# Decode attention on one core: one head at a time in shared 4 MB slots, V stationary in the value matmul, wq loaded first and wo last

## The chip, the cores and the metric

The kernel runs on one core of a Trainium2 chip. The metric is the device time in microseconds of one execution, the median of several. All runs quoted here are of the state "fast" unless it is said otherwise. Clocks, waits and packet times come from the one run of each kernel that was profiled. Abbreviations: PE is TensorE, PEld its weight loads, DVE is VectorE, ACT is ScalarE, POOL is GpSimd, SP is SyncE, which only issues loads here. "PEclk" is the clock that TensorE was granted, as a share of full speed.

## The reference, cut to what matters

```python
def reference(x, k_cache, v_cache, wq, wo, w1, w2, w3, w4):   # names shortened
    # B=2, Sq=1, D=512; Hq=32 query heads, Hkv=8 key heads (rep=4), Sk=32768, Dh=128, F=1792
    xn = layernorm(x)
    q  = (xn @ wq).reshape(B, 1, 32, 128)
    p  = softmax(q . k_cache * 128**-0.5)          # per head, over 32768 keys
    s  = (p @ v_cache) @ wo
    h2 = gelu(layernorm(xn) @ w3) @ w4             # the w1/w2 part shifts its one row away
    return x + s * silu(xn + h2)
```

K and V are 268.4 MB of bf16. Every element is used once for four query rows, so the kernel is a stream of loads with a little arithmetic behind each of them. One thing about correctness has to be known: the attention output is so small beside x that the comparison with the reference says little about the attention part.

## The kernel before

Heads are handled in pairs, and K and V arrive in tiles of 4096 tokens: 1 MB, 8 KB in a row on each of 128 partitions.

```python
NC_MAX = 4096; GPS = 2; TPB = 8        # tokens per tile, heads at a time, K tiles per PSUM tile
KN_BUFS = 5; V_BUFS = 6
...
kn = kn_pool.tile([128, TPC, 128], BF16, tag="kn", name=f"kn{j}")
k_eng.dma_start(out=kn[:, :, :],
    in_=A_k_cache[b, g, c * NC:(c + 1) * NC, :].rearrange("(p t) d -> p t d", p=128))
...
for c in range(NCHUNK + 1):
    # 1. transpose K of chunk c on TensorE, copy PSUM to SBUF (DVE 3 of 4, ACT 1 of 4)
    nc.tensor.transpose(out=tTs[j][:, i, :], in_=kns[j][:, u, :], identity=ident[:, :])
    ...
    # 2. PV of chunk c-1: exp columns stationary (4), V moving (128 columns), two heads in turn
    nc.tensor.matmul(o_ps[j][32 * j:32 * j + rep, 0:Dh],
        lhsT=pep[j][:, u * rep:(u + 1) * rep], rhs=pvt[j][:, u, :],
        start=first, stop=last, tile_position=(0, 32 * j))
    ...
    # 3. scores of chunk c: K^T stationary, q moving (4 columns); then exp on ACT
    nc.tensor.matmul(scs[j][:, u * rep:(u + 1) * rep],
        lhsT=ktbs[j][blk][:, i, :], rhs=q4[j], start=True, stop=True)
```

wq, w3 and w4 are loaded after the first K and V tiles, wo in two halves in the second and third of eight sets of heads; wq and wo in rows of 1 KB.

The softmax here doesn't subtract the row's maximum and nothing guards it: scores larger than these inputs give would overflow.

Of the kernel before, what the change touches and what calls it, by code (L numbers as in the profile page):

```python
# [8 lines left out]
F32 = mybir.dt.float32  # L10
BF16 = mybir.dt.bfloat16
ACT = mybir.ActivationFunctionType
ALU = mybir.AluOpType

NC_MAX = 4096
GPS = 2
TPB = 8
KN_BUFS = 5
V_BUFS = 6
KT_BUFS = 12  # L20
EP_BUFS = 4
TT_BUFS = 3
SC_BUFS = 2
O_BUFS = 2
# [3 lines left out]
def kernel(  # L28
# [13 lines left out]
    dbg: bass.AP | None = None,  # L42
# [9 lines left out]
    assert Sq == 1 and Dh == 128 and rep == 4 and D % 128 == 0 and Fdim % 128 == 0  # L52
    assert Hkv % GPS == 0
    DK = D // 128
    FK = Fdim // 128
    NC = min(NC_MAX, Sk)
    assert Sk % NC == 0
    TPC = NC // 128
    assert TPC % TPB == 0
    NBLK = TPC // TPB  # L60
    NCHUNK = Sk // NC
    eps = 1e-5
    inv_sqrt_dh = float(Dh) ** -0.5
    GELU_C = 0.7978845608028654

    n_sets = B * (Hkv // GPS)

    pers = ctx.enter_context(tc.tile_pool(name="pers", bufs=1))
    kn_pool = ctx.enter_context(tc.tile_pool(name="kn", bufs=KN_BUFS))
    v_pool = ctx.enter_context(tc.tile_pool(name="vpool", bufs=V_BUFS))  # L70
    pro_ps = ctx.enter_context(tc.tile_pool(name="pro_ps", bufs=1, space=bass.MemoryType.PSUM))
    tT_psp = ctx.enter_context(tc.tile_pool(name="tT_ps", bufs=TT_BUFS, space=bass.MemoryType.PSUM))
    sc_psp = ctx.enter_context(tc.tile_pool(name="sc_ps", bufs=SC_BUFS, space=bass.MemoryType.PSUM))
    o_psp = ctx.enter_context(tc.tile_pool(name="o_ps", bufs=O_BUFS, space=bass.MemoryType.PSUM))

    def set_groups(s):
        b = s // (Hkv // GPS)
        g0 = (s % (Hkv // GPS)) * GPS
        return b, [g0 + j for j in range(GPS)]

    def issue_chunk_dma(s, c, k_eng=None, v_eng=None):
        b, groups = set_groups(s)
        k_eng = k_eng or nc.sync
        v_eng = v_eng or nc.sync
        kns, vts = [], []
        for j in range(GPS):
            g = groups[j]
            kn = kn_pool.tile([128, TPC, 128], BF16, tag="kn", name=f"kn{j}")
            k_eng.dma_start(
                out=kn[:, :, :],  # L90
                in_=A_k_cache[b, g, c * NC:(c + 1) * NC, :].rearrange("(p t) d -> p t d", p=128),
            )
            kns.append(kn)
        for j in range(GPS):
            g = groups[j]
            vt = v_pool.tile([128, TPC, 128], BF16, tag="v", name=f"vt{j}")
            v_eng.dma_start(
                out=vt[:, :, :],
                in_=A_v_cache[b, g, c * NC:(c + 1) * NC, :].rearrange("(p t) d -> p t d", p=128),
            )  # L100
            vts.append(vt)
        return kns, vts

    x_bf = pers.tile([B, D], BF16)
    nc.sync.dma_start(out=x_bf[:, :], in_=A_x[:, 0, :])

    first_dma = issue_chunk_dma(0, 0, k_eng=nc.sync, v_eng=nc.sync)
# [4 lines left out]
    def layernorm(dst_f32, src_f32, tagp):  # L112
        stats = pers.tile([B, nc.vector.BN_STATS_DIM], F32, name=f"stats_{tagp}")
        nc.vector.bn_stats(out=stats[:, :], in_=src_f32[:, :])
        mv = pers.tile([B, nc.vector.BN_AGGR_DIM], F32, name=f"mv_{tagp}")
        nc.vector.bn_aggr(out=mv[:, :], in_=stats[:, :])
        rstd = pers.tile([B, 1], F32, name=f"rstd_{tagp}")
        nc.vector.tensor_scalar_add(out=rstd[:, :], in0=mv[:, 1:2], scalar1=eps)
        nc.scalar.activation(out=rstd[:, :], in_=rstd[:, :], func=ACT.Sqrt)
        nc.vector.reciprocal(out=rstd[:, :], in_=rstd[:, :])  # L120
        nc.vector.tensor_scalar(
            out=dst_f32[:, :], in0=src_f32[:, :],
            scalar1=mv[:, 0:1], scalar2=rstd[:, 0:1],
            op0=ALU.subtract, op1=ALU.mult,
        )
# [10 lines left out]
    ident = pers.tile([128, 128], BF16)  # L136
    make_identity(nc, ident[:, :])
    ones_f = pers.tile([128, 1], F32)
    nc.gpsimd.memset(ones_f[:, :], 1.0)

    treg = pro_ps.tile([128, 2 * DK * B], BF16, tag="pro")
    for k in range(DK):
        nc.tensor.transpose(out=treg[:, k * B:k * B + B], in_=xn_bf[0:B, k * 128:(k + 1) * 128], identity=ident[0:B, 0:B])  # L143
        nc.tensor.transpose(out=treg[:, (DK + k) * B:(DK + k) * B + B], in_=ln2_bf[0:B, k * 128:(k + 1) * 128], identity=ident[0:B, 0:B])
    xT = pers.tile([128, 2 * DK, B], BF16)
    nc.vector.tensor_copy(out=xT[:, :, :], in_=treg[:, :].rearrange("p (k b) -> p k b", b=B))

    wo_sb = pers.tile([128, Hq, D], BF16)
    w3_sb = pers.tile([128, DK, Fdim], BF16)
    w4_sb = pers.tile([128, FK, D], BF16)  # L150
# [4 lines left out]
    o_sb = pers.tile([36, Dh], BF16)  # L155
    nc.gpsimd.memset(o_sb[:, :], 0.0)
    s_acc = [pers.tile([128, rep], F32, name=f"s_acc{j}") for j in range(GPS)]

    QPH = 4 if Hq % 4 == 0 else 2
    NQP = Hq // QPH  # L160
    wq3 = A_wq.rearrange("(k p) f -> p k f", p=128)
    wqp = tc.alloc_tile_pool(name="wq_pool", bufs=NQP)
    qT_ps = pro_ps.tile([128, Hq * B], F32, tag="pro")
    for hp in range(NQP):
        wq_sb = wqp.tile([128, DK, QPH * Dh], BF16, tag="wq")
        nc.sync.dma_start(out=wq_sb[:, :, :], in_=wq3[:, :, hp * QPH * Dh:(hp + 1) * QPH * Dh])  # L166
        for hh in range(QPH):
            h = hp * QPH + hh
            for k in range(DK):
                nc.tensor.matmul(  # L170
                    qT_ps[:, h * B:(h + 1) * B],
                    lhsT=wq_sb[:, k, hh * Dh:(hh + 1) * Dh],
                    rhs=xT[:, k, :],
                    start=(k == 0), stop=(k == DK - 1),
                )
    nc.vector.tensor_copy(out=q_sb[:, :, :], in_=qT_ps[:, :].rearrange("p (h b) -> p b h", b=B))  # L176
    wqp.release()
    nc.sync.dma_start(out=w3_sb[:, :, :], in_=B_w3.rearrange("(k p) f -> p k f", p=128))
    nc.sync.dma_start(out=w4_sb[:, :, :], in_=B_w4.rearrange("(f p) d -> p f d", p=128))

    kt_pool = ctx.enter_context(tc.tile_pool(name="ktb", bufs=KT_BUFS))
    ep_pool = ctx.enter_context(tc.tile_pool(name="ep", bufs=EP_BUFS))
    rec_pool = ctx.enter_context(tc.tile_pool(name="rec", bufs=4))
    part_pool = ctx.enter_context(tc.tile_pool(name="part", bufs=4))

    def emit_mlp_branch():
        hT_ps = pro_ps.tile([128, FK * B], F32, tag="pro")
        for f in range(FK):
            for k in range(DK):
                nc.tensor.matmul(  # L190
                    hT_ps[:, f * B:(f + 1) * B],
                    lhsT=w3_sb[:, k, f * 128:(f + 1) * 128],
                    rhs=xT[:, DK + k, :],
                    start=(k == 0), stop=(k == DK - 1),
                )
        hf = pers.tile([128, FK * B], F32)
        nc.vector.tensor_copy(out=hf[:, :], in_=hT_ps[:, :])
# [10 lines left out]
        h2_ps = pro_ps.tile([B, D], F32, tag="pro")  # L208
        for f in range(FK):
            nc.tensor.matmul(  # L210
                h2_ps[0:B, :],
                lhsT=h_bf[:, f * B:(f + 1) * B],
                rhs=w4_sb[:, f, :],
                start=(f == 0), stop=(f == FK - 1),
            )
        t_f = pers.tile([B, D], F32)
        nc.vector.tensor_add(out=t_f[:, :], in0=xn[:, :], in1=h2_ps[0:B, :])
# [4 lines left out]
    emit_mlp_branch()  # L222

    for s in range(n_sets):
        b, groups = set_groups(s)
        wo3 = A_wo.rearrange("(h p) d -> p h d", p=128)
        if s == min(1, n_sets - 1):
            nc.sync.dma_start(out=wo_sb[:, 0:Hq // 2, :], in_=wo3[:, 0:Hq // 2, :])
        if s == min(2, n_sets - 1):
            nc.sync.dma_start(out=wo_sb[:, Hq // 2:Hq, :], in_=wo3[:, Hq // 2:Hq, :])  # L230
        q4 = [q_sb[:, b, groups[j] * rep:(groups[j] + 1) * rep] for j in range(GPS)]
        o_ps = [o_psp.tile([128, Dh], F32, tag="o", name=f"o_ps{j}") for j in range(GPS)]
        for j in range(GPS):
            nc.vector.memset(s_acc[j][:, :], 0.0)  # L234


        prev = None
        for c in range(NCHUNK + 1):
            if c < NCHUNK:
                if s == 0 and c == 0:  # L240
                    kns, vts = first_dma
                else:
                    kns, vts = issue_chunk_dma(s, c)

                ktbs = [[None] * NBLK for _ in range(GPS)]
                for blk in range(NBLK):
                    tTs = [tT_psp.tile([128, TPB, 128], BF16, tag="tT", name=f"tT{j}{blk}") for j in range(GPS)]
                    for i in range(TPB):
                        u = blk * TPB + i
                        for j in range(GPS):  # L250
                            nc.tensor.transpose(out=tTs[j][:, i, :], in_=kns[j][:, u, :], identity=ident[:, :])  # L251
                    for j in range(GPS):
# [130 lines left out]
```

## Time and profile before

| | before |
|---|---|
| time, median of 3 (range) | 698.43 us (698.17 to 698.53) |
| TensorE busy | 84% of the span |
| load queue, share of the 16 DMA engines | 97.1% |
| steady load rate | 423 to 425 GB/s |

These are lines of the page of the kernel before. In PEclk and GB/s each entry is one of 40 equal slices of the span (17.4 us). The queue lines give packets, MB and the share of 16 DMA engines. The line after the heading of part 4 is the chain of waits, followed back from the last instruction.

```profile
span 696.8 us, 26830 instructions
...
PE 586.2 (84%) x12566; PEld 541.8 (78%) x12566; DVE 332.3 (48%) x729; ACT 171.2 (25%) x264; POOL 0.9 (0%) x8
...
PEclk9999998999979999999999999999999999999999
...
GB/s 341 389 423 424 423 419 408 426 424 424 411 410 426 423 424 425 422 425 424 424 424 425 424 424 424 418 412 404 423 423 421 412 425 422 412 398 424 422 338 14
...
q1 hardware_dynamic: 47560, 280.52, 97.1%
q8 instruction: 98, 1.61, 0.8%
...
PE 46%; DMA 35%; DVE 9%; ACT 6%; SPq 2%; issue 2%; ACTq 0%; DVEq 0%
```

The loads run at 423 to 425 GB/s with dips, and the rate falls in the last two slices. Queue 8 is not data: it is TensorE fetching its own program, 98 packets of 16 KB. The program has 12,566 matmuls and as many weight loads, so a packet holds about 256 instructions. The chain is shared between PE and DMA, so neither is far from the limit.

The timeline of the kernel before shows the two shapes of matmul that matter, eight scores and then a run of PV (start, length, engine, line, operation; "128x4" and "128x128" are what the matmul streams):

```profile
300.03 0.35 PE L284 MATMUL sc_6436<-q_sb,ktb_6369 128*128 128x4 bf16 x8
300.32 1.00 PE L266 MATMUL o_ps_6099<-vt_6279,ep_6501 128*4 128x128 bf16 x15
```

The length of a group contains the latency of its last matmul, about 0.2 us. Without it, scores follow each other 26 ns apart and the PV matmuls of this group about 55 ns apart.

### The profile page before, as it was taken

Reading aid. Unit: us, or ns where it says so; the run is one execution under the profiler, and the core shown is the slowest. Engines: PE = TensorE matmul, PEld = TensorE weight load, DVE = VectorE, ACT = ScalarE, POOL = GpSimd, SP = SyncE. Lnnn points to the kernel's source line nnn. Section 1 sums busy time; section 2 is a strip of 40 time slices with the busy share of each in tenths; the row PEclk is TensorE's granted clock in tenths of the full one; section 3 lists DMA queues with packets and bytes.
Section 4 is the critical chain, followed back from the end, with each engine's and each line's share of the span. In section 5 each row is a group of like instructions: output and inputs, shape, how many; then the busy total and the mean of one; then the engine's idle time right before and its main releaser. Section 6 shows DMA issues by size and latency. Waiting matters only on the chain.

```text
span 696.8 us, 26830 instructions
## 1 busy us (share of the span) xinstructions
PE 586.2 (84%) x12566; PEld 541.8 (78%) x12566; DVE 332.3 (48%) x729; ACT 171.2 (25%) x264; POOL 0.9 (0%) x8
## 2 busy tenths in 40 slices
PE   2688886889858898899889888888898888899887
PEld 2568886878858888788878878887887888788884
DVE  2245553445534554455545544553555454445542
ACT  0232221222202222222212222221222222122220
POOL 0000000000000000000000000000000000000000
PEclk9999998999979999999999999999999999999999
DMA  8999999999999999999999999999999999999980
GB/s 341 389 423 424 423 419 408 426 424 424 411 410 426 423 424 425 422 425 424 424 424 425 424 424 424 418 412 404 423 423 421 412 425 422 412 398 424 422 338 14
DMA packets 47671, 282.23 MB, mean 405 GB/s; under 512 B 4292, under 2 KB 14280, under 8 KB 14792
## 3 DMA queue, kind: packets, MB, share of 16 engines
q1 hardware_dynamic: 47560, 280.52, 97.1%
q8 instruction: 98, 1.61, 0.8%
q14 instruction: 13, 0.11, 0.0%
HBM read 280.50 MB, written 0.00 MB: 403 GB/s over the span
## 4 chain that ended last, share of the span: by engine, by line
PE 46%; DMA 35%; DVE 9%; ACT 6%; SPq 2%; issue 2%; ACTq 0%; DVEq 0%
DMA kn_9125<-in_A_k_cache_dram 2%; DMA kn_12933<-in_A_k_cache_dram 2%; DMA kn_10557<-in_A_k_cache_dram 2%; DMA kn_5553<-in_A_k_cache_dram 2%; DMA kn_3412<-in_A_k_cache_dram 2%; DMA kn_7693<-in_A_k_cache_dram 2%; DMA kn_15309<-in_A_k_cache_dram 2%; DMA kn_8653<-in_A_k_cache_dram 2%; DMA kn_3884<-in_A_k_cache_dram 2%; DMA kn_9597<-in_A_k_cache_dram 2%; DMA kn_2940<-in_A_k_cache_dram 2%; DMA kn_7221<-in_A_k_cache_dram 2%; DMA kn_14837<-in_A_k_cache_dram 2%; SPq L166 2%; DMA kn_4201<-in_A_k_cache_dram 2%
## 5 line engine op out<-in xcount | busy, mean ns | idle before, releaser
L170 PE MATMUL qT_ps<-xT,wq_sb 128*128 128x2 bf16 x128 | 4.7, 166 | 10.8 <-DMA wq_sb<-in_A_wq_dram 10.8
L170 PEld LDWEIGHTS <-wq_sb 128*128 128x128 bf16 x128 | 4.0, 105 | 11.6 <-DMA wq_sb<-in_A_wq_dram 11.6
L326 PE MATMUL oT_ps<-ident,o_sb 36*128 36x36 bf16 x8 | 1.5, 188 | 10.8 <-DVE o_sb L319 10.8
L326 PEld LDWEIGHTS <-o_sb 36*128 36x128 bf16 x8 | 0.7, 93 | 11.6 <-DVE o_sb L319 11.6
L176 DVE CAST q_sb<-qT_ps 128x64 bf16<-128x64 f32 x1 | 0.2, 225 | 17.0 <-PE qT_ps L170 17.0
L251 PEld LDWEIGHTS <-kn_4199 128*128 128x128 bf16 x32 | 3.9, 146 | 4.9 <-DMA kn_4199<-in_A_k_cache_dram 4.9
L234 DVE MEMSET s_acc_138<- 128x4 f32 x8 | 0.5, 62 | 14.6 <-PE S_ps L308 11.8
L336 PE MATMUL s_ps<-wo_sb,oT_sb 128*2 128x512 bf16 x32 | 7.1, 379 | 0.3 <-DVE oT_sb L329 0.3
L255 ACT COPY ktb_439<-tT_420 128x1024 bf16<-128x1024 bf16 x1 | 1.0, 1012 | 22.4 <-PE tT_420 L251 22.4
L251 PEld LDWEIGHTS <-kn_2294 128*128 128x128 bf16 x32 | 3.6, 135 | 3.8 <-DMA kn_2294<-in_A_k_cache_dram 3.8
L336 PEld LDWEIGHTS <-oT_sb 128*2 128x2 bf16 x32 | 2.6, 84 | 4.4 <-DVE oT_sb L329 0.4
L251 PEld LDWEIGHTS <-kn_80 128*128 128x128 bf16 x32 | 3.3, 136 | 3.0 <-DMA kn_80<-in_A_k_cache_dram 1.7
L143 PE MATMUL treg<-ident,xn_bf 2*128 2x2 bf16 x4 | 0.4, 166 | 5.7 <-DVE xn_bf L132 5.7
L251 PE MATMUL tT_4207<-ident,kn_4199 128*128 128x128 bf16 x8 | 1.0, 308 | 4.8 <-DMA kn_4199<-in_A_k_cache_dram 4.8
L143 PEld LDWEIGHTS <-xn_bf 2*128 2x128 bf16 x4 | 0.3, 102 | 5.7 <-DVE xn_bf L132 5.7
L255 ACT COPY ktb_4249<-tT_4230 128x1024 bf16<-128x1024 bf16 x1 | 1.0, 1012 | 14.1 <-PE tT_4230 L251 14.1
L251 PEld LDWEIGHTS <-kn_12933 128*128 128x128 bf16 x32 | 3.1, 120 | 1.5 <-DMA kn_12933<-in_A_k_cache_dram 1.5
L255 ACT COPY ktb_2344<-tT_2325 128x1024 bf16<-128x1024 bf16 x1 | 1.0, 1012 | 12.9 <-PE tT_2325 L251 12.9
L251 PEld LDWEIGHTS <-kn_4201 128*128 128x128 bf16 x32 | 3.8, 142 | 0.5 <-DMA kn_4201<-in_A_k_cache_dram 0.5
L251 PE MATMUL tT_2302<-ident,kn_2294 128*128 128x128 bf16 x8 | 1.0, 311 | 3.7 <-DMA kn_2294<-in_A_k_cache_dram 3.7
L343 DVE TENSOR_TENSOR sg<-s_ps,g_sb 2x512 f32<-2x512 f32 x1 | 0.7, 679 | 7.2 <-PE s_ps L336 7.2
L251 PEld LDWEIGHTS <-kn_10557 128*128 128x128 bf16 x32 | 3.2, 122 | 1.0 <-DMA kn_10557<-in_A_k_cache_dram 1.0
(2872 smaller groups left out, 2158.1 us busy)
## 6 DMA issues: line engine op xcount, KB each, us to landing
wq_sb<-in_A_wq_dram SPq DMA_DIRECT2D x8, 512.0 KB, 8.9
wo_sb<-in_A_wo_dram SPq DMA_DIRECT2D x2, 2048.0 KB, 23.6
w_sb<-in_B_w_dram SPq DMA_DIRECT2D x2, 1792.0 KB, 16.1
kn_78<-in_A_k_cache_dram SPq DMA_DIRECT2D x1, 1024.0 KB, 4.9
kn_80<-in_A_k_cache_dram SPq DMA_DIRECT2D x1, 1024.0 KB, 7.0
vt_82<-in_A_v_cache_dram SPq DMA_DIRECT2D x1, 1024.0 KB, 9.0
vt_84<-in_A_v_cache_dram SPq DMA_DIRECT2D x1, 1024.0 KB, 11.0
kn_561<-in_A_k_cache_dram SPq DMA_DIRECT2D x1, 1024.0 KB, 17.4
```

What stands on the lines that cost most here:

```text
L143: nc.tensor.transpose(out=treg[:, k * B:k * B + B], in_=xn_bf[0:B, k * 128:(k + 1) * 128], identity=ident[0:B, 0:B])
L166: nc.sync.dma_start(out=wq_sb[:, :, :], in_=wq3[:, :, hp * QPH * Dh:(hp + 1) * QPH * Dh])
L170: nc.tensor.matmul(qT_ps[:, h * B:(h + 1) * B], lhsT=wq_sb[:, k, hh * Dh:(hh + 1) * Dh], rhs=xT[:, k, :], start=(k == 0), stop=(k == DK - 1),)
L176: nc.vector.tensor_copy(out=q_sb[:, :, :], in_=qT_ps[:, :].rearrange("p (h b) -> p b h", b=B))
L234: nc.vector.memset(s_acc[j][:, :], 0.0)
L251: nc.tensor.transpose(out=tTs[j][:, i, :], in_=kns[j][:, u, :], identity=ident[:, :])
L255: nc.scalar.copy(out=ktb[:, :, :], in_=tTs[j][:, :, :])
L326: nc.tensor.transpose(out=oT_ps[:, 0:nrows], in_=o_sb[0:nrows, 0:Dh], identity=ident[0:nrows, 0:nrows])
L336: nc.tensor.matmul(s_ps[0:B, :], lhsT=oT_sb[:, h, :], rhs=wo_sb[:, h, :], start=(h == 0), stop=(h == Hq - 1),)
L343: nc.vector.tensor_tensor(out=sg[:, :], in0=s_ps[0:B, :], in1=g_sb[:, :], op=ALU.mult)
```

## The change

The intent is fewer and longer transfers, and a cheaper PV. One head is handled at a time. K, V, wq, w3 with w4, and wo share five slots of 32 KB per partition. One item of work is half a sequence of one head: a 4 MB load of K and one of V, 128 tiles of each; there are 32 items. PV has V stationary and streams the four exp columns. wq comes first in long rows, wo last.

```diff
-NC_MAX = 4096
-GPS = 2
-KN_BUFS = 5
-V_BUFS = 6
+KPT = 128
+SLOTS = 5
 ...
+    def slot(name):
+        return slots.tile([128, SLOT], BF16, tag="slot", name=name)      # SLOT = KPT * Dh
+    def load_cache(cache, b, g, i, name):
+        t = slot(name)
+        nc.sync.dma_start(out=t[:, :],
+            in_=cache[b, g, i * NK:(i + 1) * NK, :].rearrange("(p t) d -> p (t d)", p=128))
+        return t
 ...
+        for blk in range(NBLK):                          # emit_k: 16 blocks of 8 tiles
+            ... 8 transposes, one copy (DVE 3 of 4, ACT 1 of 4)
+            if blk >= 2:
+                scores(blk - 2, done[blk - 2])
+        for blk in (NBLK - 2, NBLK - 1):
+            scores(blk, done[blk])
+        nc.scalar.activation(out=ep[:, :], in_=sc[:, :], func=ACT.Exp, scale=inv_sqrt_dh)
 ...
-                        nc.tensor.matmul(o_ps[j][32 * j:32 * j + rep, 0:Dh],
-                            lhsT=pep[j][:, u * rep:(u + 1) * rep], rhs=pvt[j][:, u, :], ...
-                            tile_position=(0, 32 * j))
+        for u in range(KPT):                             # emit_v
+            nc.tensor.matmul(o[:, :],
+                lhsT=vt[:, u, :], rhs=ep[:, u * rep:(u + 1) * rep], ...)
 ...
+    wo_parts = [(0, 16), (16, 28), (28, 32)]
+    for n in range(NW):
+        ep = emit_k(n)
+        if n == 0:
+            emit_mlp()
+        if n + 1 < NW:
+            k_tiles[n + 1] = load_cache(A_k_cache, *work[n + 1], "k")
+            v_tiles[n + 1] = load_cache(A_v_cache, *work[n + 1], "v")
+        else:
+            ... wo into a slot, in three parts
+        emit_v(n, ep)
```

## The prediction

> **What bounds the kernel now.** The loads. The page gives 282.2 MB at a mean of 405 GB/s and queue 1 at 97.1% of the DMA engines; slices without a dip run at 423 to 425. TensorE is close behind: the chain of waits shows 9.46 us per 4 MB where compute sets the pace and 9.9 us where DMA does. Lost besides: (a) about 3.4 us before the first data; (b) dips to 387-413 GB/s at set ends and where 1 KB-row weights load (queue's own waits: twice 14.7 us for scores); (c) the tail: 301, then 215 GB/s from 670 to 680 us, last load about 683 us, then the last PV, 7.1 us of output projection and 3.5 us to the end (windows, timeline).
>
> **Costs from the packet records.** An 8 KB packet takes 309 ns and the next on its engine starts 306 ns after it; 1 KB packets move at about 388 GB/s, 42 ns each. That fits 0.0368 ns per byte plus about 5 ns per packet. [...]
>
> **What the change does.**
> 1. K and V come in 32 KB packets: 512 instead of 2048 per engine; 1536 x 5 ns = 7.5 us less on the critical resource. wq, w3 and w4 become long rows: about 2 us. Fewer semaphore packets: about 1 us. wo stays in 1 KB rows.
> 2. PV keeps V stationary and streams 4 columns. PV matmuls are now 54 ns apart; scores, which have the new PV's shape, 26 ns. TensorE then needs per 8 MB item 128 x (55 + 26 + 26) = 13.7 us plus 2-3 us of bubbles (no interleaving now), against 19.4 us of loading. DVE needs about 10 us. All have slack, so the faster PV alone buys nothing; it pays for the lost interleaving.
> 3. A load waits for the tile five loads earlier, whose use must end within about four transfers (39 us) of landing; compute needs under 20. The queue should not run dry: the dips at set ends (about 5 us) and the tapered tail go.
> 4. wo comes last; its 4 MB hides the last K and V work. The tail after the last load falls from about 13.6 us to 8: a few output matmuls (3 us), then the 3.5 us end.
>
> **Sum.** Per engine: bytes 644.5 us, packets 4, semaphores 0.5, instruction fetch 5.7 (98 packets x 939 ns / 16): 655. Plus 0.6% for the noise of steady slices (424 where this sum gives 427): 659. Start 3.4 and tail 8: 670; plus 1.6 between span and time: 671 us (-3.9%).
>
> Range 661 to 681. Faster by over 2%: 0.93; within 2%: 0.06; slower by over 2%: 0.01.
>
> **What would show it.** Step 1: 32 KB packets of about 1210 ns, steady slices at 427-430 GB/s. Step 2: TensorE busy well below 84%, idle before each item waiting for K; DMA most of the chain. Step 3: no slice but first and last below 420. Step 4: last load within 9 us of the end.
>
> **What would make it wrong.** 32 KB packets no faster, or split (then about 679); instruction fetch stuck behind 1.2 us packets, starving TensorE; the new PV slower than the scores; slots freed too late (bubbles over 6 us per item).

The paragraph on packet costs: the two figures there follow from the two packet sizes of the kernel before: (306 - 42) ns over 7168 bytes is 0.0368 ns per byte, and about 5 ns are left for each packet.

## The result, and the profile after

The changed kernel takes 687.52 us (685.06 to 691.73, four runs; the profiled one is the fastest of them). The ratio to the kernel before is 0.9853, 95% interval 0.9821 to 0.9886: within 2%. Ratios here are the mean time of one kernel's fast runs over that of the other's in the same rounds, so they are not quite the ratio of the medians quoted. The prediction was 671 us, range 661 to 681: too fast by 16.5 us, out of its range.

The lines of the page after that answer to those shown of before:

```profile
span 683.3 us, 26445 instructions
...
PE 562.9 (82%) x12590; PEld 538.2 (79%) x12590; DVE 296.7 (43%) x473; ACT 155.0 (23%) x168; POOL 0.8 (0%) x7
...
PEclk9977777777777777777787777877777777877778
...
GB/s 370 428 429 429 432 431 430 427 425 428 429 424 427 434 426 427 430 427 432 429 427 426 427 427 430 427 429 428 428 425 429 434 429 428 427 429 424 404 233 97
...
q1 hardware_dynamic: 13800, 280.50, 96.3%
q8 instruction: 98, 1.61, 1.0%
...
PE 56%; DMA 31%; issue 6%; ACT 6%; SPq 0%; DVE 0%; ACTq 0%
```

The steady rate is what was predicted (427 to 430), and the dips are gone. Three things were not predicted: the granted clock fell from 0.97 to 0.77, the chain is now mostly PE, and the last three slices fall to 404, 233 and 97 GB/s.

One item, from the timeline after (one PV phase, then the start of the next K):

```profile
229.59 3.48 PE L244 MATMUL o<-ep,v 128*128 128x4 bf16 x127 [0.69 <-ACT ep L226]
234.53 0.19 PE L244 MATMUL o<-ep,v 128*128 128x4 bf16 x1 [1.45 <-issue]
...
235.00 2.72 PE L213 MATMUL tT<-ident,k 128*128 128x128 bf16 x24
...
237.77 1.01 PE L213 MATMUL tT<-ident,k 128*128 128x128 bf16 x8
...
240.88 0.61 PE L213 MATMUL tT<-ident,k 128*128 128x128 bf16 x8
```

Three readings. PV is as fast as predicted: 127 matmuls in 3.48 us, 26 ns apart. It stops 1.45 us before its last matmul, with "issue" as the cause: TensorE waits for nothing that the profile shows, and in this trace such a stall ends about 1.4 us after a fetch packet of queue 8 has landed (median 1.40 us over the 38 stalls of TensorE longer than 0.3 us). And the first 24 transposes after PV take 2.72 us, 107 ns apart, eight of them 1.01 us; 5 us later eight take 0.61 us (55 ns apart). The windows view of the same item shows why (window, us, then busy us and instructions of PE, PEld, DVE, ACT, POOL, then PEclk, DMA share, GB/s):

```profile
225.00:230.00 5.00, 3.65 (x97) 3.41 (x95) 2.45 (x4) 2.48 (x3) 0.00 (x0) 1.00 1.02 436
230.00:235.00 5.00, 3.55 (x121) 3.47 (x117) 0.26 (x1) 0.00 (x0) 0.00 (x0) 0.54 0.99 423
235.00:240.00 5.00, 5.00 (x67) 5.00 (x68) 2.53 (x6) 1.01 (x1) 0.00 (x0) 0.50 0.98 416
240.00:245.00 5.00, 5.00 (x118) 4.96 (x116) 3.94 (x6) 1.16 (x2) 0.00 (x0) 0.94 0.97 419
```

About a microsecond into PV the clock drops to half and stays there for about 10 us. It does so in nearly every item. The next item begins 20.0 us later (its PV starts at 249.58), while 8.4 MB at 429 GB/s take 19.6 us.

The waits of TensorE after (us in total, times, longest):

```profile
PE o L244 <- issue: 25.2, 23, 2.6
PE o L244 <- ACT ep L226: 22.1, 31, 1.6
PE sc L205 <- ACT ktb L216: 19.6, 29, 0.9
PE tT L213 <- issue: 13.3, 12, 2.0
PE tT L213 <- DMA k<-in_A_k_cache_dram: 8.1, 9, 2.0
```

All waits for "issue" together are 43.9 us after and 0.2 us before. Waits for K are only 8.1 us (besides 7.4 for the first K): TensorE had no slack left.

The end of the run, windows after:

```profile
632.00:649.00 17.00, 15.01 (x341) 14.56 (x341) 8.80 (x13) 4.64 (x5) 0.00 (x0) 0.80 0.99 404
649.00:666.00 17.00, 14.96 (x306) 14.38 (x304) 8.16 (x12) 4.09 (x5) 0.00 (x0) 0.76 0.61 233
666.00:683.00 17.00, 12.44 (x162) 6.88 (x161) 2.39 (x5) 0.56 (x1) 0.00 (x0) 0.80 0.31 102
```

From 649 us on, only 61% of the DMA engines' time is used, although wo is queued. The packet records say when things ended: the last packet of K or V at 661.2 us, the last of wo at 673.7, the span at 683.3. The records do not name the engine of a packet, but they show how many packets of K and V are under way at once: 16 until 640 us, 7 to 9 from 646 to 660. So about eight of the 16 engines are done with K and V some 12 us before the others.

Which of these moments does the end hang on? The chain of waits between 630 and 684 us (start, length, what) has only one load in it, the last K, and ends with the 32 output matmuls; in it and after them no engine waits for wo:

```profile
610.75 41.22 DMA k<-in_A_k_cache_dram
...
671.52 8.35 PE s_ps L283 x32
```

The last K landed at 652.0 us. The 31.3 us from there to the end are work: 18.8 us for the last item, then the output matmuls and the end.

So there are three suspects for 16.5 us: the half clock, the stalls of instruction fetch, and loads that end late on some engines.

### The profile page after: what moved, and what is told of

Its sections match the earlier page's. It is cut to its first block, busy times and chain, and to the rows that moved or that the text cites. A ratio compares the mean times of both kernels' runs of the same rounds, so it can differ in the third digit from the quotient of the medians.

```text
span 683.3 us, 26445 instructions
## 1 busy us (share of the span) xinstructions
PE 562.9 (82%) x12590; PEld 538.2 (79%) x12590; DVE 296.7 (43%) x473; ACT 155.0 (23%) x168; POOL 0.8 (0%) x7
## 3 DMA queue, kind: packets, MB, share of 16 engines
q8 instruction: 98, 1.61, 1.0%
## 4 chain that ended last, share of the span: by engine, by line
PE 56%; DMA 31%; issue 6%; ACT 6%; SPq 0%; DVE 0%; ACTq 0%
PE tT L213 32%; DMA k<-in_A_k_cache_dram 31%; PE o L244 12%; PE sc L205 10%; ACT ktb L216 3%; ACT ep L226 2%; PE s_ps L283 1%; PE S L253 1%; ACT L226 0%; SPq L72 0%; DVE sg L290 0%; DVE out_bf L292 0%; SPq L93 0%; SPq L92 0%; ACTq L216 0%
## 5 line engine op out<-in xcount | busy, mean ns | idle before, releaser
L213 PE MATMUL tT<-ident,k 128*128 128x128 bf16 x3968 | 355.7, 247 | 21.5 <-issue 13.3
L218 DVE COPY ktb<-tT 128x1024 bf16<-128x1024 bf16 x384 | 260.7, 692 | 217.0 <-PE tT L213 216.8
L213 PEld LDWEIGHTS <-k 128*128 128x128 bf16 x3968 | 283.0, 112 | 25.4 <-issue 16.4
L216 ACT COPY ktb<-tT 128x1024 bf16<-128x1024 bf16 x128 | 129.5, 1012 | 485.8 <-PE tT L213 485.8
L205 PE MATMUL sc<-q_sb,ktb 128*128 128x4 bf16 x4096 | 180.4, 166 | 23.2 <-ACT ktb L216 19.6
L205 PEld LDWEIGHTS <-ktb 128*128 128x128 bf16 x4096 | 160.3, 99 | 30.4 <-ACT ktb L216 22.5
L244 PE MATMUL o<-ep,v 128*128 128x4 bf16 x3968 | 112.9, 166 | 47.5 <-issue 25.2
L244 PEld LDWEIGHTS <-v 128*128 128x128 bf16 x3968 | 111.1, 102 | 51.6 <-issue 51.6
L238 DVE TENSOR_REDUCE s<-ep 128x4 f32<-128x512 bf16 x32 | 22.0, 686 | 70.5 <-ACT ep L226 70.5
L226 ACT ACTIVATE ep<-sc 128x512 bf16<-128x512 f32 x32 | 19.1, 597 | 15.9 <-PE sc L205 15.9
```

What stands on the lines that cost most here:

```text
L205: nc.tensor.matmul(sc[:, u * rep:(u + 1) * rep], lhsT=ktb[:, j, :], rhs=q4, start=True, stop=True,)
L213: nc.tensor.transpose(out=tT[:, j, :], in_=kt[:, blk * TPB + j, :], identity=ident[:, :])
L216: nc.scalar.copy(out=ktb[:, :, :], in_=tT[:, :, :])
L218: nc.vector.tensor_copy(out=ktb[:, :, :], in_=tT[:, :, :])
L226: nc.scalar.activation(out=ep[:, :], in_=sc[:, :], func=ACT.Exp, scale=inv_sqrt_dh)
L238: nc.vector.tensor_reduce(out=state["s"][:, i, :], in_=ep[:, :].rearrange("p (t h) -> p h t", h=rep), axis=AX.X, op=ALU.add,)
```

## The experiments

Eighteen kernels were run, each beside the kernel before on the same chip. The table gives medians; clock and last packet are those of the profiled run. Where an expectation names a theory by a letter, A is "the granted clock follows the columns streamed, and a phase of 4-column matmuls lowers it", F is "instruction fetch sets the pace", B the rival of A that dense weight loads lower the clock, and C the rival that the clock is low only because TensorE stands idle. For F the trace of the changed kernel gives: of 97 intervals between the fetch packets of queue 8, 90 are longer than 6.0 us and the shortest is 5.3, while 127 PV matmuls with their weight loads, about one packet's worth, ran in 3.48 us. Nearly all started from the changed kernel; the edits are shown against it, or against the kernel named.

| run | edit in short | time us (median) | ratio to before | clock | last K or V packet, us |
|---|---|---|---|---|---|
| changed kernel | | 687.52 | 0.9853 | 0.770 | 661.2 |
| e1_wide64 | PV streams 64 columns | 683.74 | 0.9787 | 0.900 | 661.3 |
| e3_8k | 4 MB loads in four 8 KB pieces | 697.2 | 0.9977 | 0.764 | 676.6 |
| e5_noload | one K and V for all (wrong) | 555.84 (one run) | | 0.864 | |
| e7_before_narrow | before, PV of 4 columns (wrong) | 716.2 | 1.0254 | 0.728 | |
| e8_inter_wide | e1, PV woven into the next K | 691.27 | 0.9892 | 0.896 | 661.7 |
| e8n_inter | the same with 4 columns | 694.58 | 0.9937 | 0.743 | 661.4 |
| e10_half | every other PV, 128 columns (wrong) | 679.37 | 0.9723 | 0.907 | 658.3 |
| e6_light | 1/8 of transposes, 1/16 of PV (wrong) | 672.1 | 0.9617 | 0.539 | 651.0 |
| e2_oldpv | PV undone | 747.29 (3 fast runs) | 1.0708 | 0.923 (slow run) | 700.6 (slow run) |
| e11_pv512 | PV of 512 columns for 4 tiles at once | 744.22 | 1.0650 | 0.99 | 701.8 |
| e12_wide_16k | e1, loads in two 16 KB pieces | 687.85 | 0.9847 | 0.918 | 667.2 |
| e13_hold | e1, part of PV held back into gaps | 687.39 | 0.9843 | 0.925 | 661.1 |
| e14_wo_early | wo before the last K and V | 696.44 | 0.9962 | 0.768 | 672.6 |
| e15_tail | e1, wo early, end reordered | 694.58 | 0.9938 | 0.906 | 673.0 |
| e16_tail_spread | e15, wo in four spread parts | 692.73 | 0.9912 | 0.906 | 673.3 |
| e17_wo_spread | changed kernel, wo in four spread parts | 697.68 | 0.9977 | 0.762 | 673.5 |
| e18_pool16 | e1, 4096 tiny instructions on GpSimd | 688.37 | 0.9853 | 0.908 | 665.1 |
| e19_pool32 | e1, 8192 of them | 712.97 | 1.0195 | 0.901 | 688.8 |

### Is it the width of PV that halves the clock?

**e1_wide64** repeats the four exp columns 16 times on the moving side, so that the same PV matmuls stream 64 columns:

```diff
-            state["o"] = o_ps.tile([128, rep], F32, tag="o", name="o")
+            state["o"] = o_ps.tile([128, WIDE, rep], F32, tag="o", name="o")      # WIDE = 16
-                rhs=ep[:, u * rep:(u + 1) * rep],
+                rhs=ep[:, u * rep:(u + 1) * rep].unsqueeze(1).to_broadcast([128, WIDE, rep]),
-                ... in0=o[:, :], in1=rec[:, :],
+                ... in0=o[:, 0, :], in1=rec[:, :],
```

> The changed kernel, but each PV matmul streams its 4 weight columns 16 times over (64 moving columns, same V weight load, same result). Theory A [...]: mean granted clock rises from 0.77 to 0.90 or more, TensorE's item falls to 16-18 us, the loads set the pace, time 667-677 us. Rival B [...]: clock stays at or below 0.77, time 687 us or more. Rival C (instruction-fetch stalls in PV leave TensorE idle, and that lowers the clock): stalls remain, so clock stays near 0.77-0.80 and time 683-690.

Measured: 683.74 us (683.61 to 686.25), ratio 0.9787 (0.9771 to 0.9803), clock 0.90. Sixteen times the streamed columns made the kernel 4 us faster. The clock is what theory A said; the time is not (667 to 677 us was expected), so on the time this is a miss. Issue waits stayed at 44 us:

```profile
PEclk9979899999999999999979998999899999988888
...
PE tT L214 <- DMA k<-in_A_k_cache_dram: 21.0, 10, 7.6
PE tT L214 <- issue: 18.5, 22, 1.9
PE sc L206 <- issue: 16.9, 21, 1.8
PE o L245 <- issue: 8.3, 8, 2.3
```

**e7_before_narrow** asks the opposite question of the kernel before: only 4 of V's 128 columns are streamed.

```diff
-                            o_ps[j][32 * j:32 * j + rep, 0:Dh],
+                            o_ps[j][32 * j:32 * j + rep, 0:4],
-                            rhs=pvt[j][:, u, :],
+                            rhs=pvt[j][:, u, 0:4],
 ...                                                      # the normalisation reads these four
```

> Wrong result on purpose: the kernel before, with only 4 of V's 128 columns streamed in each PV matmul. Nothing else changes and TensorE has less to do. Theory A: the clock falls from 0.97 to 0.60-0.85, and the time does not fall: 690-715 us. Rivals B and C: weight loads and fetches are as before, so the clock stays over 0.95 and the time is the same or 1% less (690-698).

Measured: 716.2 us (712 to 720), ratio 1.0254 (1.0237 to 1.0271). Less work and 18 us more. Its page:

```profile
PE 627.2 (87%) x12566; PEld 585.2 (82%) x12566; DVE 336.8 (47%) x729; ACT 171.2 (24%) x264; POOL 0.9 (0%) x8
...
PEclk9976766667666777887778676666778776666767
```

The clock falls from 0.97 to 0.73 and TensorE is busy for 41 us more. This shows the effect in a kernel that has nothing else of the change. It also ends rival B: e1_wide64 kept its weight loads and regained the clock, and this kernel has no more of them than before and lost it.

The records of the granted clock in the traces before and after show how it moves. They have two levels only, 1.0 and 0.5 (transposes 55 and 107 ns apart), and every stretch at one level, but for the last, is a whole number of windows of 3.413 us (67 stretches in the changed kernel, 17 in the kernel before). Counting matmuls per window of that grid: in the changed kernel all 18 windows with nothing but PV matmuls of 4 columns, 27 to 116 of them, are followed by half clock; in the kernel before the four windows with 51 to 58 PV matmuls of 128 columns and at most four others are followed by full clock. TensorE counts as "busy" in the profile in both (in the changed kernel 3.55 of 5 us in the stretch from 230 us above, mostly PV at a clock of 0.54; in the kernel before 16.49 of 20 us from 400 to 420 us, at 1.00). At half clock, windows of the changed kernel with 3,180 streamed columns or more, most of them with 24 to 30 transposes, are followed by full clock, and windows with 3,164 or fewer by half. It holds beyond them: in the windows between 60 and 600 us of all 20 traces, about 3,100, the clock after a window of 3,300 or more streamed columns was always full, after one of fewer than 2,800 always half, and a line at 3,150 sorts 98% of them (313 of the 314 of these two kernels). The narrow PV is not alone in this. The window before the drop in the item shown, 227.0 to 230.4 us, holds 4 transposes, 24 scores and 32 PV matmuls, 736 columns: the gaps at the end of the K phase count too.

**e3_8k** cuts each cache load into four pieces of 8 KB per partition:

```diff
-        nc.sync.dma_start(out=t[:, :], in_=cache[b, g, i * NK:(i + 1) * NK, :].rearrange(...))
+        src = cache[b, g, i * NK:(i + 1) * NK, :].rearrange("(p t) d -> p (t d)", p=128)
+        for c in range(0, SLOT, PIECE):                   # PIECE = 4096
+            nc.sync.dma_start(out=t[:, c:c + PIECE], in_=src[:, c:c + PIECE])
```

> The changed kernel with each 4 MB cache load cut into four of 1 MB, so packets of 8 KB again. Rival C: the waits of TensorE put down to issue fall from 44 us to under 10, and with them the clock recovers to over 0.90; time 676-682 us (the loads' pace at 424 GB/s). Theory A: the issue waits may fall too, but the clock stays at 0.74-0.80; item about 18.5-19.5 us, so loads and TensorE nearly balance; time 678-686. If 32 KB packets have nothing to do with the issue waits they stay at 40 us or more, and time is 687 or more.

Measured: 697.2 us, ratio 0.9977, clock 0.764, steady rate 418 to 419 GB/s, issue waits 5.4 us, waits for K 37.2 us. On the time this is a miss: 678 to 686 us was theory A's range.

```profile
PEclk9977777777777777777777777777777777787776
...
PE o L244 <- issue: 5.4, 9, 1.0
```

Two things follow. The clock is as low without fetch stalls, so C falls. And almost the whole gain of the change hangs on the 32 KB packets: with everything else of it in place the time is that of the kernel before. A caution: 8 KB pieces at a pitch of 32 KB ran at 418 to 419 GB/s, while the contiguous 1 MB tiles of the kernel before reached 424. Why was not tested.

### Is TensorE's pace set by its instruction fetch?

**e5_noload** uses one K and one V tile for all items, so nothing loads after the start.

```diff
-            k_tiles[n + 1] = load_cache(A_k_cache, *work[n + 1], "k")
-            v_tiles[n + 1] = load_cache(A_v_cache, *work[n + 1], "v")
+            k_tiles[n + 1] = k_tiles[0]
+            v_tiles[n + 1] = v_tiles[0]
```

> Wrong result on purpose: the changed kernel with only the first K and V tile loaded and used for all 32 items, so no cache traffic. Theory A: the clock stays at 0.85 or below with nothing to wait for; the item is 18-19.5 us and the span 610-640 us; issue waits fall below 10 us, since the fetches have the DMA engines to themselves. Rival C: no fetch stalls, so the clock is over 0.92, the item about 16 us and the span 545-570. If issue waits stay at 40 us, they do not come from sharing the DMA engines.

Measured (one run, state unknown): 555.84 us, clock 0.864, and the list of TensorE's matmul waits has none for issue. Without traffic, fetches cost TensorE next to nothing: a fetch packet starts about 1 us after TensorE has used up a block, against about 3.6 us in the changed kernel (estimates from the packets' times and a count of 256 instructions to a block, since no record says where a block ends), and blocks come as close as 3.6 to 4.5 us where under load they hardly come closer than 6 us (7 of 97 intervals in the changed kernel). The time lies in rival C's range (545 to 570 us) and the clock in neither's. But the scheduler ordered TensorE's work differently here, PV of one item between the scores of the next, so the time decides nothing between A and C; e3_8k does.

**e8_inter_wide** and **e8n_inter** weave PV of the previous item, eight at a time, between the transposes of the next, with 64 and with 4 columns, so that the pace of instructions is even (the edit in words; TensorE's order is pinned as well, in e13_hold too):

```diff
-    emit_v: for u in range(KPT): nc.tensor.matmul(o, lhsT=vt[:, u, :], ...)
+    emit_k: after each block of transposes and scores: pv(blk)    # 8 PV of the item before
```

> Both suspected causes taken away, right result: the 64-column PV of the first experiment, and its matmuls of one item woven between the transposes of the next item, 8 and 8, in pinned order. Theory A+F [...]: blocks are now alike, so the issue waits fall from 44 us to under 20, the clock is 0.90 or more, TensorE waits for K and V and the loads set the pace: 668-680 us. If it stays at 683 or more, something else binds.

> The same weave with 4-column PV. Theory A: at the loads' pace only 22 transposes of 128 columns fall in each 3.4 us window, under the 25 or so that kept the clock up in both traces, so the clock sinks to 0.5-0.7, a block of 128 pairs takes 6.5-7 us, the item 20.3-21 us, and the time is 695-712 us, slower than the unwoven changed kernel. If only idle time and fetch stalls lowered the clock, it is 0.9 or more and the time 668-680.

Measured: 691.27 us (ratio 0.9892, clock 0.896) and 694.58 us (691.4 to 696.7; ratio 0.9937, clock 0.743). Both are worse than what they started from. Issue waits did not fall but rose to 75 us in the wide one, where under 20 was expected: a miss. The narrow one lies just outside theory A's ranges (clock 0.5 to 0.7, 695 to 712 us) and far from the other theory's (0.9, 668 to 680). An even mix does not help; that the blocks of 256 instructions are then used up about as fast as they can be fetched would explain it, and was not tested apart.

**e10_half** does every other PV matmul, each 128 columns wide: as many streamed columns as e1_wide64, half the PV instructions.

```diff
-        for u in range(KPT):
+        for u in range(0, KPT, 2):                        # WIDE = 32: 128 columns each
```

> Wrong result on purpose: the 64-column kernel (684 us, issue waits 44 us), but with every other PV matmul left out and the rest made twice as wide (128 columns), so moving columns and array time of PV stay as they were and 128 of 776 matmul-or-weight-load pairs' instructions per item go. Theory F: 2.5 instead of 3 blocks per item, issue waits fall to under 20 us, the loads set the pace, 668-679 us. If instruction fetch does not bind, 681-686.

Measured: 679.37 us (679.1 to 679.8), ratio 0.9723 (0.9709 to 0.9738): 4.4 us below e1_wide64. Its page and waits:

```profile
q8 instruction: 82, 1.34, 0.8%
...
PE tT L214 <- DMA k<-in_A_k_cache_dram: 55.6, 25, 7.7
PE tT L214 <- issue: 7.3, 9, 1.4
PE sc L206 <- issue: 6.5, 10, 1.0
```

Issue waits fall from 44 to 14 us, as F says. But TensorE now waits 55.6 us for K. What it saved in stalls it mostly spends waiting for data. Between the profiled runs the span is 6.4 us shorter than that of e1_wide64: the last K lands 2.9 us earlier, and the way from there to the end is 3.5 us shorter.

**e12_wide_16k** is e1_wide64 with loads in two pieces of 16 KB rows (the edit of e3_8k with PIECE = 8192).

> The version with 64-column PV, and each 4 MB cache load cut into two pieces of 16 KB per partition, so that instruction fetches share the DMA engines with shorter packets. If the packet in front of a fetch sets the fetch's latency: TensorE issue waits fall from 44 us to under 30 us, load rate about 424 to 427 GB/s, 680 to 684 us. If the fetch waits stay above 35 us and the rate falls, 684 to 690 us, and the size of the packets is not what the fetch stalls hang on. Clock 0.88 to 0.93 in both.

Measured: 687.85 us, ratio 0.9847; a miss, since its fetch waits fell below 30 us but the time did not.

```profile
PE o L245 <- issue: 3.0, 3, 1.2
...
PE tT L214 <- DMA k<-in_A_k_cache_dram: 56.3, 33, 2.8
```

Issue waits went from 44 to 5.8 us and the kernel became 4 us slower, with 423 to 427 GB/s. This is the run that made me doubt my theory: the fetch stalls of TensorE are not all that the time hangs on. It is not a clean test, though. Its loads were slower (last K or V packet 5.9 us later than in e1_wide64), and the end followed that packet after 18.8 us instead of 23.1, so fewer stalls may have gained some 4 us that the loads took away again.

**e13_hold** is e1_wide64 with the last 40 PV matmuls of an item held back and run in the gaps at the end of the next item's K phase.

```diff
+        held(KPT - HOLD, KPT - HOLD + 16)                 # before the last two score blocks
         for blk in (NBLK - 2, NBLK - 1):
             scores(blk, done[blk])
+        held(KPT - HOLD + 16, KPT)                        # while ACT does the exp
```

> The version with 64-column PV, where the last 40 PV tiles of each item are held back and run in the gaps at the end of the next item's K phase (16 before the last two score blocks, 24 after). If the gaps at the end of K and the clock set the pace: clock at or above 0.93, the ACT waits of K's end gone, 678 to 683 us. If the instruction fetch sets the pace: the filled gaps come back as issue waits (over 44 us), 683 to 690 us.

Measured: 687.39 us, clock 0.925. The ACT waits at the end of K shrank from 39 to 7.6 us, waits for K grew to 70.4 us, and the last K or V packet came at 661.1 us, as in the two kernels before it. The time lies in the range of the second expectation, but not by its mechanism: issue waits were 44.7 us, as before (43.7), and the filled gaps came back as waits for K.

### What sets the end of the loads?

Set side by side, the changed kernel, e1_wide64 and e13_hold let TensorE wait 8, 21 and 70 us for K in mid-run, so their TensorE pace differs, but their last K or V packet comes at 661.2, 661.3 and 661.1 us; in e8_inter_wide and e8n_inter it is 661.7 and 661.4. The loads, not TensorE, set that moment. They do not set the time alone. The last K lands at 651.9 to 652.3 us in all five, and from there to the end of the span it is 31.3 us in the changed kernel, 32.4 in e1_wide64, 35.0 in e13_hold, 37.2 in e8_inter_wide and 40.1 in e8n_inter: that part is TensorE's.

**e6_light** keeps all loads and takes nearly all work away: 1/8 of the transposes, 1/16 of PV.

```diff
-        for blk in range(NBLK):          # transposes
+        for blk in range(2):
-        for u in range(KPT):             # PV
+        for u in range(0, KPT, 16):
```

> Wrong result on purpose: the changed kernel's loads in full, but an eighth of the transposes and a sixteenth of the PV matmuls, so TensorE has about 5 us of work per item and 40 instead of 98 instruction blocks to fetch. It shows the floor of the loads. As predicted at first (fetches spread evenly over the engines, tail hidden by wo): the floor is 670 us minus 3. Theory G (the traces show half of the engines finishing their K and V packets 10-14 us before the others, which fits 98 fetches of 1.07 us on 8 engines): the skew shrinks to 4-7 us, the last K or V packet ends at 650-654 us instead of 658-661, and the time is 667-673 us. If the floor is 677 or more, the loads themselves and not TensorE cost most of the missing gain.

Measured: 672.1 us (671.4 to 672.4), ratio 0.9617. That was the time predicted for the change, in a kernel that does little but load.

```profile
GB/s 373 430 427 423 435 431 433 432 422 433 433 431 433 425 429 431 429 437 427 425 433 431 433 433 423 429 435 428 435 425 432 431 429 434 427 429 434 427 345 139
...
q8 instruction: 40, 0.66, 0.4%
```

The steady rate is hardly higher than in the changed kernel, but it holds one slice longer. Fetches fell from 98 to 40. The last K or V packet against the number of fetches: 98 gives 661.1 to 661.7 us (five kernels), 82 gives 658.3, 40 gives 651.0. That is 0.18 us per fetch, while one fetch packet of 1.07 us shared evenly over 16 engines would be 0.067 us. At that point it was a correlation: e6_light and e10_half also gave TensorE less to do.

**e18_pool16** and **e19_pool32** test it by adding fetches without touching TensorE. GpSimd, otherwise idle, gets 4096 or 8192 memsets of one element that nobody needs (the same element in e18_pool16, 64 in turn in e19_pool32); TensorE's order is the same instruction by instruction as in e1_wide64.

```diff
     for n in range(NW):
+        for _ in range(128):                              # e19_pool32: 256, junk[:, u % 64:u % 64 + 1]
+            nc.gpsimd.memset(junk[:, :], 0.0)
         ep = emit_k(n)
```

> The version with 64-column PV and 4096 memsets of one element on the otherwise idle GpSimd, which nothing waits for: 16 more instruction fetches, TensorE's order the same. The last packet of wo came at 674 us in three kernels with 98 fetches, at 671.2 with 82 and at 662.4 with 40: 0.17 to 0.20 us a fetch. If the fetches themselves hold up the loads wherever they come from: last K or V packet 3 us later (661.3 to about 664.3), time 686 to 688 us. If a fetch costs only its share of 16 engines (0.067 us): about 662.4, 684 to 686. If it is not the fetches but TensorE's pace behind them that set the end: no later than 661.5.

> The same with 8192 memsets, 32 more fetches: last K or V packet 6 us later (about 667) and 689 to 692 us if every fetch costs 0.17 to 0.20 us; 663.4 and 685 to 687 us if it costs its share of 16 engines; 661.5 and no change if fetches do not matter to the loads. If GpSimd itself takes longer than the kernel, only the packet times count.

Measured: e18_pool16 688.37 us (687.0 to 689.2), 4.6 us above e1_wide64, its last K or V packet at 665.1 us, 3.8 us later. e19_pool32 712.97 us (707.0 to 715.2), last K or V packet at 688.8 us. From the page and groups of e18_pool16:

```profile
q14 instruction: 42, 0.34, 0.1%
...
L270 POOL MEMSET junk<- 1x1 f32 x4096 | 365.5, 89 | 236.1
```

In e1_wide64 queue 14 has 11 packets and 0.08 MB. My expectation counted blocks of 256 instructions; GpSimd fetches blocks of half that size, so these are 31 more packets and 0.26 MB, and the prediction of 3 us for "16 fetches" met 3.8 us. 0.26 MB is 0.6 us of this load rate. The fetches cost the loads about six times their bytes. In e19_pool32, 63 more packets cost 27.5 us, far beyond both expectations. There the loss lies where GpSimd works, and GpSimd itself waited 80 us for its own fetches:

```profile
POOL 8777777777777777777700000000000000000000
...
GB/s 376 417 438 420 428 431 421 426 432 421 427 432 407 398 413 412 347 390 360 409 361 428 420 424 423 426 423 420 429 426 426 418 412 433 418 436 424 392 86 97
```

The fetches cause the delay: that is shown. How they do it can be read from the packet records. A packet starts within some 15 ns of the end of the one before it on its engine, so packets can be put in chains, one for each engine (in the changed kernel 908 of 985 loads' shares could be; where several packets end together, a chain may change over to another engine).

- **What a fetch costs its engine.** One engine's share of a 4 MB load, eight packets, takes 9.71 us without a fetch among them (818 cases in the changed kernel) and 11.26 us with one (82 cases). So a fetch of TensorE costs 1.55 us: its own packet of 1.07, and about 0.5 by which the data packet after it is longer, 1.71 instead of 1.21 us.
- **Where TensorE's fetches fall.** On a chain that has them, the next is nearly always the eighth after the last: in 51 of 57 steps in the changed kernel, in all 47 in e10_half. In the changed kernel five chains of 45 to 61 loads have none. So eight engines take all of them, about 12 each, and 12 x 1.55 us = 19 us on each of the eight.
- **Why that delays the loads.** A 4 MB load is complete only when its slowest engine is done: the last K landed at 652.0 us, when about eight engines had been through with K and V since 646. One fetch then costs 1.55 / 8 = 0.19 us of loading, an estimate that meets the 0.18 measured. In mid-run the other engines work ahead as far as the five slots allow, which is why the share stays at 1.0 and the lag shows at the end, as engines that have nothing left to do.
- **Why 63 fetches of GpSimd cost so much more than 31.** They fall on one chain, not among the eight: in e19_pool32, 50 of them in 26 successive loads, 0.7 us each. As an estimate, 31 cost that engine about 22 us, hardly more than the 19 us of TensorE's eight, and 63 cost it about 44, which is 25 us more. Measured were 3.8 and 27.5 us. The slices of 347 to 413 GB/s in e19_pool32 are then the other engines waiting for this one.

The memsets might also disturb something other than DMA; e1_wide64 and e18_pool16 have the same TensorE busy time within 1% (561.1 and 556.8 us), which speaks against it, and so does the 1.55 us, which stands beside the fetch packets themselves in a kernel without memsets.

### Was the new PV needed, and was wo last right?

**e2_oldpv** undoes PV alone: exp stationary, V moving, one head at a time.

```diff
-                lhsT=vt[:, u, :], rhs=ep[:, u * rep:(u + 1) * rep],
+                lhsT=ep[:, u * rep:(u + 1) * rep], rhs=vt[:, u, :],
```

> The changed kernel with PV undone: the 4 exponential columns stationary, 128 columns of V moving, one head at a time. Theory A: clock 0.92 or more. Work of an item at that clock is about 19.3 us without stalls. Theory F: the transposing blocks (5.2 us) still stall, so the item is 20-20.5 us and the time 684-694, no better than the changed kernel in spite of the clock. Without F: 674-682.

Measured: 747.29 us (three fast runs, 744.0 to 753.3), ratio of fast runs 1.0708. A miss: I expected it near the changed kernel because the clock would stay up. The clock did (0.93 to 0.94 in the fast runs), but in the profiled run these PV matmuls start 67 ns apart on average (56 at full clock, 107 where it is halved after the gap for the exp), against 40 ns in the kernel before, where two heads alternate between two column positions and part of the matmuls start together. (The profiled run, 756.8 us, is slow; the times of fast runs alone are compared.) With one head at a time and full width, V as the stationary side was the faster one.

**e11_pv512** streams four V tiles, 512 columns, against 16 stationary exp columns, woven into the next K; three quarters of the result is thrown away.

> A version meant to beat both, right result: 32 KB packets and shared slots as in the changed kernel, but PV takes 4 tiles at once (16 exponential columns stationary, 512 columns of V moving, the diagonal blocks kept), woven between the next item's transposes; last V in four pieces. 64 instead of 256 PV instructions per item: about 75 blocks in all. Theories A and F: clock over 0.9, TensorE 17-18 us per item at 2.3 blocks of 6.1 us (14 us), so it waits for K; loads set the pace; 672-680 us. If it is over 684 another limit of TensorE is at work.

Measured: 744.22 us, ratio 1.065, clock 0.99, TensorE busy 92%. A miss: a pair of these matmuls took 530 ns to the transposes after it (219 to the second, 311 after that), where two of the 512-column output matmuls, 216 ns apart, would take 432. An item took about 22 us, and a full clock could not make up for it.

**e14_wo_early** moves wo before the last K and V, nothing else; **e17_wo_spread** does it in four parts of 1 MB, one ahead of each of the last four cache loads.

```diff
+            if n + 1 == NW - 1:
+                ... wo into a slot, in three parts
             k_tiles[n + 1] = load_cache(A_k_cache, *work[n + 1], "k")
             v_tiles[n + 1] = load_cache(A_v_cache, *work[n + 1], "v")
-        else:
-            ... wo into a slot, in three parts
```

> The changed kernel with one part undone in kind: wo is loaded before the last K and V instead of after them; nothing else differs. If wo last hides work of the tail as the prediction's step 4 says: the last K or V packet comes about 9 us later than 661 us and the end of PV with it, so 692 to 697 us, with the last PV and the 32 output matmuls (8 us) all after the last load. If wo last hides nothing, because TensorE sets the end either way: 685 to 690 us.

> The changed kernel with wo in four 1 MB parts ahead of the last four cache loads, everything else as it was. If wo last hides work (the prediction's step 4) even without a blocked issue: 690 to 694 us. If the 9 us of the earlier run came from the blocked issue alone: 686 to 689 us.

Measured: 696.44 us (696.3 to 696.8), as expected if wo last hides work, and 697.68 us (697.0 to 697.9), later than both of its expectations. That is 9 to 10 us worse than the changed kernel. Windows of e14_wo_early:

```profile
632.00:649.00 17.00, 14.86 (x341) 14.29 (x341) 9.01 (x15) 4.64 (x5) 0.00 (x0) 0.80 0.69 245
649.00:666.00 17.00, 4.33 (x70) 4.24 (x71) 1.35 (x2) 0.00 (x0) 0.00 (x0) 0.50 1.04 424
666.00:683.00 17.00, 15.23 (x368) 13.67 (x366) 7.83 (x14) 4.64 (x5) 0.00 (x0) 0.80 0.28 119
```

In the first window the engines are a third idle, because the second of the three issues of wo held the load queue for 31 us, and the last K and V were issued behind it, at 646.6 and 648.0 us; in the second TensorE has little to do; in the third it catches up with no loads to hide behind. In e17_wo_spread the longest issue held the queue for 12 us, and the time was no better. wo last is right, by 9 to 10 us. Not told apart is how much of that is hiding and how much is that wo, loaded early, takes one of five slots away from K and V.

**e15_tail** and **e16_tail_spread** try to better the end from e1_wide64: wo early (in three parts, or spread), 28 of the 32 output matmuls before the last PV, and the last V in four pieces.

> The version with 64-column PV; wo before the last K and V, 28 of the 32 output matmuls before the last PV, the last V in four pieces. If the order of the end is what costs (8 us of output matmuls after the last PV, wo in short rows on half idle DMA engines): 675 to 681 us, with the last PV within 7 us of the end. If the uneven finish of the DMA engines sets the end (last K or V packet at about 671 us): 680 to 686 us.

> As the run before with the same end (64-column PV, 28 output matmuls before the last PV, last V in four pieces), but wo in four 1 MB parts, one ahead of each of the last four cache loads, so that no issue of wo should hold the load queue up. If the blocked issue (31 us) cost the 11 us of that run: no PE wait for K over 3 us at the end, DMA at 400 GB/s or more until the last K or V, 676 to 682 us. If the load rate falls again before the last V: 685 us or more.

Measured: 694.58 and 692.73 us against 683.74. e15_tail missed both its ranges. e16_tail_spread missed the hoped-for 676 to 682 us and meets its other case: the DMA share fell to 0.68 between 615 and 632 us, before the last V. The time from the end of the last PV to the end did shrink, from 12.5 us in the changed kernel to 5.6, but the last K or V packet came at 673 us. An end that is neater for TensorE is worth nothing when it makes the last load later.

## Why the prediction was wrong, point by point

The profiled run after gives the parts. The prediction had the last load at 659 + 3.4 = 662.4 us and 8 us of tail. Measured were 673.7 us (the last packet of wo) and 9.6 us. That is 11.3 us for the loads and 1.6 us for the tail. The profiled run is the fastest of four, 2.5 us below the median, and the prediction's sum was rounded down by about 1 us; together that is the 16.5 us. Since no engine waited for wo, this is a way of counting; the wait that counts is for the last K. It landed at 652.0 us, and at 641.8 in e6_light, whose last packet of wo, at 662.4, came when the prediction had it. That is the same 10 us. The rest, 2 to 3 us, is TensorE: 18.8 us for the last item where the sum of step 2 gives 16 to 17.

1. **Step 1, 32 KB packets: right.** The packets took 1214 ns (median; about 1210 was predicted), steady slices 427 to 430 GB/s. e3_8k puts it at about 14 us of loading (last wo packet at 687.9 us with 8 KB pieces, 673.7 with 32 KB).
2. **Step 2, "All have slack": wrong.** 13.7 us and 2 to 3 of bubbles were to make an item; it took 20.0 us. The half clock adds 2 to 3 us (some 40 transposes at 107 instead of 55 ns are 2.1 us, and the scores between them are slower too), fetch stalls about 1.4 us (43.9 us over 32 items), the gaps at the end of K 1.4 us. TensorE was busy for 82% of the span, not "well below 84%". TensorE came to the pace of the loads, and the chain of waits turned to PE. What that costs in time is smaller than it looks: e1_wide64, which repairs the clock, has a median 3.8 us lower, but its loads end at the same moment.
3. **Step 3, "the dips at set ends (about 5 us) and the tapered tail go": half wrong, and this is the costly half.** The dips went. The tapered tail stayed: 404, 233 and 97 GB/s. I read the taper of the kernel before as slots freed too late. In the changed kernel it is the eight engines with fetches that finish late; the taper of the kernel before was not tested apart.
4. **The Sum, "instruction fetch 5.7 (98 packets x 939 ns / 16)": the term that was mis-sized.** It shared the fetches evenly over 16 engines at 0.94 us each. They fall on eight engines and cost each of these 1.55 us. Kernels with 98, 82 and 40 fetches give 0.18 us of loading for each, so about 17 us for 98 instead of 5.7. The difference of about 12 us is the 11.3 us by which the loads were late. The two runs with fetches added on GpSimd show that the fetches are the cause.
5. **Step 4, wo last hides the tail: right in kind, 1.6 us off.** e14_wo_early and e17_wo_spread put it at 9 to 10 us. The "few output matmuls" were all 32, 8.3 us, after the last PV, because they stand last in TensorE's order.

The prediction named "instruction fetch stuck behind 1.2 us packets, starving TensorE" among what could make it wrong. It did starve TensorE (43.9 us of stalls), but that is not where most of the time went: e12_wide_16k took those stalls away and was no faster, though with slower loads. The fetches did most of their harm on the side of the loads.

What stays open: what the stalls of TensorE cost by themselves; how much of the 4 us between the changed kernel and e1_wide64 is clock, since the profiled runs (685.06 the fastest of one, 686.25 the slowest of the other) do not show it; why the changed kernel scatters over 6.7 us where e1_wide64 has three of four runs within 0.2 us; and what parts the 9 us of wo early.

The best correct version is e1_wide64, 683.74 us: 2.1% below the kernel before (the interval, 0.9771 to 0.9803, lies on both sides of 2%) and, by the medians of runs on different rounds, 0.5% below the change. Nothing built on it was faster.

## What to carry to other kernels

Count instructions as traffic where loads fill the DMA engines: here a program of 25,000 TensorE instructions was a second stream of loads (98 packets, 1.61 MB), and each fetch cost the data almost three times its even share, because the fetches fell on half of the engines and the slowest engine counts (0.18 us instead of 0.067). Look at the granted clock where matmuls stream few columns: here repeating a narrow operand to 64 columns was 16 times the streaming, and it raised the clock from 0.77 to 0.90 and was still 4 us faster. And do not read the share of an engine in the chain of waits as what a fix of that engine will gain; when two engines are level, compare when the other one ends.
